# Accumulating SBUF-to-SBUF transfers described in pieces of 1024 bytes instead of 4096

## The chip, the cores and the metric

The kernel runs on one core of one Trainium2 chip. The metric is the device time of one execution in microseconds (us); the kernel before has a median of 198.1 us over 3 runs (198.0 to 198.31).

## What is computed

One transformer layer over 2048 positions of width 512, in bfloat16:

```
h  = x + A(layernorm(x))          # attention with 32 heads of 16
h2 = h + B(layernorm(h))          # gated MLP, 512 -> 1376 -> 512: (relu(gate) * up) @ W_down

A: q, k, v = x @ wqkv
   position s sees the 8 positions s, s-2, s-4, ..., s-14 (those below 0 are masked)
   logits[s, w] = q[s] . k[s - 2w] / 4 ;  attn = softmax over the 8 shifts w
   o[s] = sum over w of attn[s, w] * v[s - 2w] ;  A = o @ wo
```

The change touches the last sum, the one over the 8 shifts.

## The kernel before, in words

The positions are worked off in four chunks of 512 (tk = 0 to 3). For each chunk:

- Layer norm 1, transposes, and the projections to q, k and v (TensorE, L559), written transposed: partitions are features, so that k and v shifted by 2w positions are the same tile read from another column.
- Scores: VectorE multiplies q by four shifted k at a time (L608, a tile "big" of 128 x 8 x 512, 8 KB in a partition); TensorE adds over the features of a head (L614); ScalarE takes the exponent (L672).
- In chunks 1 to 3 the weights are divided by their sum (L716) and then spread to all features of a head by 8 transfers on SyncE's DMA queue, from tile ex to a big tile (L732). Chunk 0 spreads them with TensorE and ScalarE (L743, L749).
- The weighted values: for each of four feature groups t, VectorE multiplies the spread weights by the 8 shifted v into a big tile mt (L764; in two halves in chunk 0, L779).
- The sum over the 8 shifts, as a tree over mt: planes 4 to 7 are added to planes 0 to 3, then 2 and 3 to 0 and 1, then 1 to 0. In chunks 0, 1 and 2 (the set DACC, all four t) the first step isn't done by VectorE, but by a transfer that GpSimd issues and that adds while it moves (L807): 4 planes x 512 x 2 bytes, 4096 bytes in each of 128 partitions, 512 KB. There are 12 of them. The rest of the tree is on VectorE (L767), and its last step writes the attention output, tile quad (L801; in chunk 0 L767 and then L771, which multiplies by the reciprocal sum). In chunk 3 the whole tree is on VectorE.
- The output projection "wo" (TensorE, L833) needs all four groups t of the chunk. Then the residual (L844, or TensorE's L836 in chunk 0), layer norm 2, the MLP (L906 up and gate, L910 and L913 evictions, L934 the product, L952 down) and the stores.

The order of the work is fixed before it runs: a planner lists each step with its engine and an estimated cost, a table RANK gives each step its place, and every engine runs its list strictly in that order, waiting at each step for the semaphores of its inputs. MLP steps of one chunk fill TensorE's list between the attention steps of the next. For a step on a DMA queue the planner holds an estimate of its own; for the transfer of L807 it is 1.0 us of GpSimd and 2.74 us of the DMA engines. For a transfer twice as large in pieces of 4096 bytes, which the code has but doesn't use here, it is 1.3 us of GpSimd and 5.48 us of the DMA engines. These constants only set the order, and the change leaves them as they are.

There are 5 big tiles. A transfer reads and writes the same one.

Of the kernel before, what the change touches and what calls it, by code (L numbers as in the profile page):

```python
# [13 lines left out]
ALU = mybir.AluOpType  # L14
# [77 lines left out]
class Plan:  # L92
# [9 lines left out]
    def add(self, key, *a, **k):  # L102
        op = Op(*a, **k)
        op.key = key
        op.seq = len(self.ops)
        if RANK:
            op.prio = RANK[op.seq]
        self.ops.append(op)
        for b in set(op.take) | set(op.use):
            b.left += 1  # L110
        return op
# [97 lines left out]
def kernel(  # L209
# [11 lines left out]
    nc = tc.nc  # L221
# [320 lines left out]
    for tk in range(NCK):  # L542
# [213 lines left out]
        for t in range(NT):  # L756
            mt = Buf(big_s)
            tpr = apr + 3 + t

            def f_mu(t=t, ab=ab, mt=mt, s0=s0):  # L760
                vb = vT[:, t, PADL + s0: PADL + s0 + CS]
                v8 = bass.AP(tensor=vb.tensor, offset=vb.offset,
                             ap=[list(vb.ap[0]), [-DIL, W]] + [list(y) for y in vb.ap[1:]])
                V.tensor_tensor(out=mt.t[:], in0=ab.t[:], in1=v8, op=ALU.mult)  # L764

            def f_a(n, mt):
                V.tensor_tensor(out=mt.t[:, 0:n, :], in0=mt.t[:, 0:n, :], in1=mt.t[:, n:2 * n, :],  # L767
                                op=ALU.add)

            def f_om(t=t, mt=mt, rc=rc, OT=OT):  # L770
                V.tensor_tensor(out=OT.t[:, t, :], in0=mt.t[:, 0, :], in1=rc.t[:], op=ALU.mult)  # L771

            vds = [vd[t], kdone.get(("v", tk - 1, t))]
            if tk in MUH:
                def f_m1(hf, t=t, ab=ab, mt=mt, s0=s0):
                    vb = vT[:, t, PADL + s0 - 4 * hf * DIL: PADL + s0 - 4 * hf * DIL + CS]
                    v4 = bass.AP(tensor=vb.tensor, offset=vb.offset,
                                 ap=[list(vb.ap[0]), [-DIL, 4]] + [list(y) for y in vb.ap[1:]])
                    V.tensor_tensor(out=mt.t[:, 4 * hf:4 * hf + 4, :], in0=ab.t[:, 4 * hf:4 * hf + 4, :], in1=v4, op=ALU.mult)  # L779

                ms = [add(("mu%d%s" % (t, "ac"[hf]), tk), "DVE", D20, lambda hf=hf, f=f_m1: f(hf),
                          [x for x in abd if x.key[0][2] == str(hf)] + vds, tpr, take=[mt], use=[ab], lat=DL) for hf in range(2)]
            else:
                ms = [add(("mu%d" % t, tk), "DVE", D40, f_mu, abd + vds, tpr, take=[mt], use=[ab], lat=DL)]
            m = ms[-1]
            if (tk, t) in PESUM:
                u = Buf(od_s)

                def f_ac(mt=mt, u=u):
                    for w in range(W):  # L790
                        nc.tensor.matmul(u.t[:], lhsT=identity[:], rhs=mt.t[:, w, :],
                                         start=(w == 0), stop=(w == W - 1))

                def f_om(t=t, u=u, rc=rc, OT=OT):
                    V.tensor_tensor(out=OT.t[:, t, :], in0=u.t[:], in1=rc.t[:], op=ALU.mult)

                m = add(("ac%d" % t, tk), "PE", 8 * MM, f_ac, [m], tpr, take=[u], use=[mt], lat=PEL)
                oev[t] = add(("om%d" % t, tk), "DVE", D5, f_om, [m, rcd], tpr, take=[OT], use=[u, rc], lat=DL)
                continue
            def f_al(t=t, mt=mt, OT=OT):  # L800
                V.tensor_tensor(out=OT.t[:, t, :], in0=mt.t[:, 0, :], in1=mt.t[:, 1, :], op=ALU.add)  # L801

            for n, du in ((4, D20), (2, D10), (1, D2)):
                f = lambda n=n, mt=mt, f=f_a: f(n, mt)
                if n == 4 and (tk, t) in DACC:
                    def f_da(mt=mt):
                        nc.gpsimd.dma_start(mt.t[:, 0:4, :], mt.t[:, 4:8, :], accum_op=ALU.add)  # L807

                    ms = [m] = [add(("ta%d" % t, tk), "POOL", 1.0, f_da, ms, tpr, use=[mt], lat=1.1, dq=(0.75, 2.74))]
                    continue  # L810
                if n == 2 and (tk, t) in DAC2:
                    def f_db(mt=mt):
                        nc.gpsimd.dma_start(mt.t[:, 0:2, :], mt.t[:, 2:4, :], accum_op=ALU.add)

                    ms = [m] = [add(("tb%d" % t, tk), "POOL", 0.95, f_db, ms, tpr, use=[mt], lat=1.1, dq=(0.75, 1.37))]
                    continue
                if n == 1 and tk in EARLY:
                    oev[t] = add(("tree%d" % t, tk), "DVE", du, f_al, ms, tpr, take=[OT], use=[mt], lat=DL)
                else:
                    ms = [m] = [add(("tree%d" % t, tk), "DVE", du, f, ms, tpr, use=[mt], lat=0.11)]  # L820
            if tk not in EARLY:
                oev[t] = add(("om%d" % t, tk), "DVE", D2, f_om, [m, rcd], tpr, take=[OT], use=[mt, rc], lat=DL)
# [199 lines left out]
```

## Time and profile before

| | |
|---|---|
| median of 3 runs | 198.1 us |
| span of the profiled execution, first to last instruction | 196.6 us |
| what lies around the span, against the median | 1.5 us |
| TensorE (PE) matmul busy | 190.5 us (97%) |
| VectorE (DVE) busy | 154.0 us (78%) |
| ScalarE (ACT) busy | 111.7 us (57%) |
| GpSimd (POOL) busy | 12.7 us (6%), 10.5 of it the 12 instructions of L807 |

The profile holds no time of its own for the profiled execution beyond its span; the 1.5 us between the span and the median of the runs are start and end, outside of what it records.

How to read the lines of the profile: each names a line of the kernel (L807), the engine, the operation, and "tile written <- tile read" with the numbers of the buffers left out. PE is the matmul side of TensorE, PEld its weight loads. POOL's busy time for a transfer is only the time that GpSimd takes to write its list of pieces (its descriptors); the data moves afterwards on 16 DMA engines, which are shared by the queue of GpSimd (q0) and the queue of SyncE (q1). "Landing" is the moment when the last of the 16 engines has reported the end. A note in square brackets at the end of a line is the time for which the engine sat idle before it, and what it waited for.

### The profile page before, as it was taken

Reading aid. Unit: us, or ns where it says so; the run is one execution under the profiler, and the core shown is the slowest. Engines: PE = TensorE matmul, PEld = TensorE weight load, DVE = VectorE, ACT = ScalarE, POOL = GpSimd, SP = SyncE. Lnnn points to the kernel's source line nnn. Section 1 sums busy time; section 2 is a strip of 40 time slices with the busy share of each in tenths; the row PEclk is TensorE's granted clock in tenths of the full one; section 3 lists DMA queues with packets and bytes.
Section 4 is the critical chain, followed back from the end, with each engine's and each line's share of the span. In section 5 each row is a group of like instructions: output and inputs, shape, how many; then the busy total and the mean of one; then the engine's idle time right before and its main releaser. Section 6 shows DMA issues by size and latency. Waiting matters only on the chain.

```text
span 196.6 us, 3034 instructions
## 1 busy us (share of the span) xinstructions
PE 190.5 (97%) x1111; PEld 97.1 (49%) x1131; DVE 154.0 (78%) x251; ACT 111.7 (57%) x234; POOL 12.7 (6%) x28
## 2 busy tenths in 40 slices
PE   7899999999999999999999999999999999999994
PEld 7756445654445434464444435444444655444542
DVE  6779999999999999999999779999686331223233
ACT  3548699984598947694334658505674615235400
POOL 4000000330000013100033000000000000000000
PEclk9999999999999999999999999999999999999999
DMA  6969980695000809947369971411002220030114
GB/s 154 310 202 389 405 262 2 122 198 108 3 0 6 196 15 173 188 89 169 81 130 198 181 204 64 82 29 24 3 0 53 53 57 0 0 107 0 27 57 133
DMA packets 21134, 21.99 MB, mean 112 GB/s; under 512 B 8736, under 2 KB 17920, under 8 KB 21120
## 3 DMA queue, kind: packets, MB, share of 16 engines
q1 hardware_dynamic: 18672, 14.65, 25.9%
q0 software_dynamic: 1728, 6.29, 17.2%
q10 hardware_dynamic: 720, 0.85, 1.4%
q8 instruction: 9, 0.15, 0.3%
q14 instruction: 5, 0.04, 0.1%
HBM read 8.42 MB, written 2.10 MB: 53 GB/s over the span
## 4 chain that ended last, share of the span: by engine, by line
PE 66%; DMA 14%; issue 13%; DVE 4%; POOL 1%; SPq 1%; POOLq 0%; DVEq 0%
PE bank L906 20%; PE bank L559 19%; PE bank L952 14%; DMA big<-big 7%; PE bank L833 5%; DMA wv_sb<-in_A_wqkv_dram 4%; PE bank L614 2%; DVE big L764 2%; PE bank L873 2%; PE bank L518 2%; DMA x_sm<-in_A_x_dram 1%; POOL big L807 1%; DMA big<-ex 1%; DVE big L608 1%; PE bank L836 1%
## 5 line engine op out<-in xcount | busy, mean ns | idle before, releaser
L906 PE MATMUL bank<-quad,wgu_sb 128*128 128x512 bf16 x313 | 72.0, 379 | 0.4
L906 PEld LDWEIGHTS <-wgu_sb 128*128 128x128 bf16 x320 | 31.0, 98 | 37.3 <-issue 0.8
L952 PE MATMUL bank<-wd_sb,gT 128*128 128x512 bf16 (+2 forms) x182 | 40.1, 366 | 0.3
L913 ACT ACTIVATE gr<-bank 128x512 bf16<-128x512 f32 x40 | 23.2, 603 | 26.0 <-PE bank L906 24.5
L910 ACT CAST up_sb<-bank 128x512 bf16<-128x512 f32 x40 | 23.2, 594 | 16.5 <-PE bank L906 14.0
L934 DVE TENSOR_TENSOR gT<-gr,up_sb 128x1024 bf16<-128x1024 bf16 x20 | 13.7, 689 | 22.7 <-ACT up_sb L910 16.8
L559 PE MATMUL bank<-quad,wqk_sb 128*128 128x512 bf16 (+1 forms) x132 | 30.2, 367 | 0.2
L952 PEld LDWEIGHTS <-gT 128*128 128x128 bf16 (+1 forms) x187 | 18.1, 98 | 19.5 <-issue 0.4
L764 DVE TENSOR_TENSOR big<-big,vT 128x4096 bf16<-128x4096 bf16 x12 | 27.0, 2283 | 0.1
L608 DVE TENSOR_TENSOR big<-quad,kT 128x4096 bf16<-128x4096 bf16 x12 | 27.0, 2284 | 0.0
L559 PEld LDWEIGHTS <-wqk_sb 128*128 128x128 bf16 x136 | 14.7, 114 | 13.0 <-issue 2.1
L963 DVE TENSOR_TENSOR row<-x_sm,bank 128x512 bf16<-128x512 bf16 (+1 forms) x17 | 10.8, 651 | 9.2 <-PE bank L952 9.2
L767 DVE TENSOR_TENSOR big<-big 128x1024 bf16<-128x1024 bf16 (+2 forms) x24 | 16.8, 729 | 1.2 <-DMA big<-big 1.2
L559 PE MATMUL bank<-quad,wv_sb 128*128 128x512 bf16 x62 | 15.7, 380 | 0.4 <-DMA wv_sb<-in_A_wqkv_dram 0.3
L807 POOL DMA_DIRECT2D big<-big x12 | 10.5, 874 | 85.0 <-DVE big L764 55.0
L833 PE MATMUL bank<-wo_sb,quad 128*128 128x512 bf16 x62 | 14.7, 379 | 0.4 <-DVE quad L801 0.3
L489 DVE TENSOR_SCALAR row<-x_sm,mv,rs 128x512 bf16<-128x512 bf16 x32 | 11.4, 407 | 1.8 <-ACT rs L471 1.8
L534 ACT COPY quad<-bank 128x1024 bf16<-128x1024 bf16 (+1 forms) x11 | 10.0, 944 | 4.5 <-PE bank L518 4.4
L567 ACT CAST kT<-bank 128x512 bf16<-128x512 f32 x16 | 8.9, 598 | 5.7 <-PE bank L559 5.5
L454 DVE BATCH_NORM_STATS2 st<-x_sm 128x6 f32<-128x512 bf16 x16 | 10.3, 675 | 2.1 <-DMA x_sm<-in_A_x_dram 2.1
L567 ACT CAST quad<-bank 128x512 bf16<-128x512 f32 x16 | 9.5, 607 | 3.6 <-PE bank L559 3.6
L443 ACT ACTIVATE row<-x_sm,mv 128x512 bf16<-128x512 bf16 x12 | 8.6, 714 | 4.2 <-DVE mv L435 4.0
(72 smaller groups left out, 157.5 us busy)
## 6 DMA issues: line engine op xcount, KB each, us to landing
big<-big POOLq DMA_DIRECT2D x12, 512.0 KB, 5.4
big<-ex SPq DMA_DIRECT2D x24, 128.0 KB, 2.7
out_dram<-row SPq DMA_DIRECT2D x15, 128.0 KB, 1.8
x_sm<-in_A_x_dram SPq DMA_DIRECT2D x3, 512.0 KB, 4.9
wgu_sb<-in_B_W_up_dram SPq DMA_DIRECT2D x1, 1376.0 KB, 8.8
wgu_sb<-in_B_W_gate_dram SPq DMA_DIRECT2D x1, 1376.0 KB, 11.8
wd_sb<-in_B_W_down_dram SPq DMA_DIRECT2D x1, 1280.0 KB, 15.2
wqk_sb<-in_A_wqkv_dram SPq DMA_DIRECT2D x2, 256.0 KB, 6.9
```

The costliest lines, as they stand in the source:

```text
L559: nc.tensor.matmul(mm.t[:, lo:hi], lhsT=wv_sb[:, dt, t:D:NT] if c == 2 else wqk_sb[:, dt, c * D + t:(c + 1) * D:NT], rhs=xnT.t[:, dt, lo:h ...
L567: nc.scalar.copy(out=o, in_=mm.t[:])
L608: V.tensor_tensor(out=pb.t[:].rearrange("p (t w) s -> p t w s", t=2), in0=q4, in1=k4, op=ALU.mult)
L764: V.tensor_tensor(out=mt.t[:], in0=ab.t[:], in1=v8, op=ALU.mult)
L767: V.tensor_tensor(out=mt.t[:, 0:n, :], in0=mt.t[:, 0:n, :], in1=mt.t[:, n:2 * n, :], op=ALU.add)
L807: nc.gpsimd.dma_start(mt.t[:, 0:4, :], mt.t[:, 4:8, :], accum_op=ALU.add)
L833: nc.tensor.matmul(od.t[:], lhsT=OT.t[:, t, j * P:(j + 1) * P], rhs=wo_sb[:, t, :], start=(t == 0), stop=(t == NT - 1 and tk not in RPE))
L906: nc.tensor.matmul(mm.t[:fs, lo:hi], lhsT=wgu_sb[:, dt, g, ft * P: ft * P + fs], rhs=hnT.t[:, dt, lo:hi], start=(dt == 0), stop=(dt == NT ...
L910: nc.scalar.copy(out=ub.t[:fs, i, :], in_=um.t[:fs, :])
L913: nc.scalar.activation(out=gr.t[:fs, i, :], in_=gm.t[:fs, :], func=ACT.Relu)
L934: V.tensor_tensor(out=gt.t[:fs, 0:n, :], in0=gr.t[:fs, 0:n, :], in1=ub.t[:fs, 0:n, :], op=ALU.mult)
L952: nc.tensor.matmul(od.t[:, c0:c1], lhsT=gts[ft].t[:fs, ft % 2, j * P:(j + 1) * P], rhs=wd_sb[:fs, ft, c0:c1], start=(ft == 0), stop=(ft == ...
```

## The change

One argument is added to the transfer. Each partition's 4096 bytes are now described as four pieces of 1024 bytes, one plane each:

```
-                        nc.gpsimd.dma_start(mt.t[:, 0:4, :], mt.t[:, 4:8, :], accum_op=ALU.add)
+                        nc.gpsimd.dma_start(mt.t[:, 0:4, :], mt.t[:, 4:8, :], accum_op=ALU.add, max_dma_last_dim=1024)
```

The instructions of all engines and their order stay the same, except that each of the 12 transfers of GpSimd is written as 128 x 4 x 512 elements where it was 128 x 2048. So a transfer has 512 pieces instead of 128, 32 for each DMA engine instead of 8. The bytes, the sum and the buffers are the same. The other place in the code that passes max_dma_last_dim isn't used.

## The prediction

> **What bounds the kernel now.** I read the busy times first, then the chain that ended last, then the DMA queues, and then the timelines of POOL, DVE and PE around the 12 transfers. From the page:
>
> ```profile
> PE 190.5 (97%) x1111; PEld 97.1 (49%) x1131; DVE 154.0 (78%) x251; ACT 111.7 (57%) x234; POOL 12.7 (6%) x28
> ...
> DVE  6779999999999999999999779999686331223233
> ...
> q0 software_dynamic: 1728, 6.29, 17.2%
> ...
> PE 66%; DMA 14%; issue 13%; DVE 4%; POOL 1%; SPq 1%; POOLq 0%; DVEq 0%
> ...
> big<-big POOLq DMA_DIRECT2D x12, 512.0 KB, 5.4
> ```
>
> PE is the bound: it idles some 6 us of the span, so almost nothing can be won anywhere. But DVE is at nine tenths or more from about 15 to 105 us, so in that stretch it has no idle time in which to absorb a delay. All 12 transfers lie there: four each issued at 34.7 to 42.2, 73.0 to 80.2 and 99.1 to 105.7 us. From the chain in order of time, the last four:
>
> ```profile
> 105.74 8.28 DMA big<-big
> 114.02 0.02 issue
> 114.04 0.70 DVE big L767
> 114.75 0.02 issue
> 114.77 0.44 DVE quad L801
> 115.20 0.05 issue
> 115.25 2.55 PE bank L833 x11
> ```
>
> The reader sees the last transfer of chunk 2 issued at 105.74, landed 8.28 us later, the rest of its tree, and wo right behind. From the timelines of DVE and of PE:
>
> ```profile
> 114.04 0.69 DVE L767 TENSOR_TENSOR big<-big 128x1024 bf16<-128x1024 bf16 x1 [1.16 <-DMA big<-big]
> ...
> 115.25 3.63 PE L833 MATMUL bank<-wo_sb,quad 128*128 128x512 bf16 x15 [0.33 <-DVE quad L801]
> ```
>
> DVE waited 1.16 us for that landing and PE 0.33 us for DVE. So here a later landing is paid by PE one for one, and an earlier one wins at most 0.33 us.
>
> In the other two chunks nothing waits yet. The slack of each transfer is the start of the addition that reads it (DVE's single instructions) minus its landing:
>
> - chunk 0: landings 39.44, 42.23, 45.09, 47.90; additions 39.86, 44.47, 47.32, 48.26; slack 0.42, 2.24, 2.23, **0.36**
> - chunk 1: landings 77.53, 80.34, 83.17, 85.98; the last addition at 86.73, slack **0.75**; the others 2.3 or more
> - between DVE's last write of the attention output and wo on PE: chunk 0, 50.62 to 50.95; chunk 1, 88.08 to 88.61. PE adds 0.3 and 0.5 of slack.
>
> In these two chunks the landings are 2.8 to 2.9 us apart, while the issues are 2.0 to 2.9 apart: from the second on, each transfer starts as the one ahead ends (first packets at 36.29, 39.00, 41.64, 44.36 in chunk 0). So within a chunk the lateness of the transfers adds up, and the fourth has the least slack.
>
> **The change, part by part.** No instruction moves on any engine; no wait is added; POOL has nothing else to do in these stretches. Two costs change.
>
> *The data, d per transfer.* In the trace's packet records an accumulating 4096-byte piece took 327 ns at the least and 340 in the median; 8 per engine and one completion of 21 ns make 2.74 us, close to the spacing seen. Plain pieces on q1 took 159 ns for 4096 bytes, 84 for 2048, 46 for 1024: a straight line of 36.8 ns per 1024 bytes and 8 to 9 ns for each piece. The 327 ns are two such readings of 4096 bytes (2 x 151) plus 26 ns. That part is paid for each piece, so a 1024-byte piece should take 2 x 37.7 + 26 = 101 ns, and with the median's 4% on top 105; 32 of them make 3.24 to 3.36 us, against 2.74: d = 0.5 to 0.6. Bounds by the nearest rows: two plain pieces of 1024 bytes, 92 ns, 2.94 us, d = 0.2; and, as the far end, the mean instead of the median of the 1024-byte pieces that spread the weights (69 ns with nothing else moving from 62 to 70 us), 2 x 69 + 26 = 164 ns, d = 2.5. Those read the same source four times over, which the transfers here don't; I take d = 0.56. Below nothing: 4 pieces can't beat two plain readings of 4096 bytes, 318 ns, so d is not under -0.18.
>
> The Trainium skill, in "DMA: Bandwidth & Descriptors", section "Why small descriptors are slow (HBM only)", speaks against this term: "SBUF↔SBUF transfers don't suffer this penalty". By that d is 0; the 46 ns for 1024 bytes against 159 for 4096 say that a fixed part of 8 ns is there on SBUF-to-SBUF pieces too, but no accumulating piece of 1024 bytes is in the trace.
>
> *The list of pieces, G.* POOL was busy 0.862 us for each list, and the first data moved 1.43 us after the start of the first list of chunks 1 and 2, thus 0.57 after its end. How much of the 0.862 goes with the number of pieces no row shows, as all 12 lists have 128. Bounds: nothing, if all of it is fixed; 3 x 0.862 = 2.59 us, if all goes with the count. The planner's own costs in the code are 1.0 us for 128 pieces and 1.3 for 256, thus 0.3 for 128 more; for 384 more that is G = 0.9, which I take. A list of 1.76 us still fits into the 2.0 to 2.9 us between issues, so G is paid once for each chunk, by its first transfer, and the others queue behind it.
>
> *The sum.* The fourth transfer of a chunk lands later by L = G + 4d = 0.9 + 2.24 = 3.14 us.
>
> - Chunk 0: DVE pays L - 0.36, about 2.8 (some of it at the first addition, 1.46 - 0.42, which also delays the fourth product by as much; the fourth transfer is queued anyway, so the sum is the same).
> - Chunk 1: the whole stretch is later by then; L - 0.75, about 2.4.
> - Chunk 2: nothing to absorb it, L, about 3.1.
>
> What one chunk leaves unused at wo on PE (0.3, 0.5) is gone at chunk 2, since there PE already waits for DVE, which carries all of it. Together 3L - 1.1 = 8.3 us. Behind chunk 2 no time is given back: PE is at nine tenths to the end and in a fixed order. Span 196.6 + 8.3 = 204.9; with the 1.5 around it, **206.4 us** against the median of 198.1.
>
> *The cover of everything else.* The SyncE queue shares the DMA engines: from 107 on the weights of chunk 3 are spread beside the third and fourth transfer of chunk 2, whose 16 completions were strewn from 111.49 to 113.66. Shorter accumulating pieces let q1 in more often. If its 32 pieces per engine (1.5 us) all go ahead, the fourth transfer loses up to 0.7 more; most of that is in the 2.2 us already, so I cost it at nothing. The reader of those weights (L764 at 119.92) isn't near wo.
>
> **The rivals.**
>
> - *Lists in proportion, 212.6 us.* With G = 2.59 POOL needs 3.45 us for a list, more than a transfer moves in 3.3, so the fourth list sets the fourth landing: 99.13 + 4 x 3.45 + 0.57 + 3.3 = 116.8, against 111.5 for the same point now, L = 5.2, 3L - 1.1 = 14.5. For it: GpSimd writes the list by program. Against: the planner's 1.0 and 1.3.
> - *Cheap pieces, 199.4 us.* G = 0 and d = 0.2 make L = 0.8: 0.4 in chunk 0, nothing left in chunk 1, 0.8 in chunk 2, 1.3 in all. For it: two readings explain all but 26 of 327 ns. With G = 0 and d = 0.56 it would be 203.7, between this and the forecast.
> - *No change, 198.1 us.* If the four pieces are joined again when the list is written, as they are contiguous in memory, or if reading them runs on without a gap, the fixed part is paid once for 4096 bytes, d = 0, and if the longer list costs nothing, L = 0. Against: every 1024-byte row on q1 is a packet of its own. The rule of the Trainium skill above, with the sentence of the same page's section "Anatomy of one DMA — SWDGE (gpsimd) path" that many descriptors can be emitted before the cost shows, gives this.
> - *Faster, 197.8 us.* Shorter pieces overlap better, one being read while the other is added: under 85 ns a piece, with G = 0, the sign turns. At the floor of 318 ns for four, L = -0.7; but only PE's 0.33 us at 115 wait for a landing at all, so that is all it wins. Place and price are bounded by that line of PE.
>
> **How the numbers follow.** Forecast, near 206.4 (204 to 210): 0.46. Lists in proportion or dearer pieces, around 212.6: 0.18. Cheap pieces, 199 to 204: 0.20. No change: 0.10. Faster: 0.06. A measurement of this kernel tells about 0.2%, 0.4 us, from no change; the fastest case is at that edge. So faster 0.05, within 0.2% 0.11, slower 0.84. The range leaves out the two last cases and a little above the list rival: 199.4 to 213.0.
>
> **What would show it.** The page's q0 line should have 512 x 12 data packets and 192 completions, 6336, and a share of 16 engines above 17.2% (about 20% of the longer span, at 105 ns a piece). POOL's L807 should take 1.7 to 1.9 us instead of 0.86; the first packet of a chunk should come by as much later. DVE's L767 should wait for "DMA big<-big" at the fourth transfer of every chunk, some 2.5 to 3 us each, where one wait of 1.16 stands now, and PE at wo for DVE quad. It is wrong if L807 stays at 0.86 us (then G = 0), if a piece takes much more than 105 ns, or if the packets stay at 1728. It is also wrong if DVE waits but PE does not: then PE had more work ready than its fixed order shows.

## The result, and the profile after

The kernel with 1024-byte pieces takes 205.32 us (median of 5 runs, 203.76 to 208.71) against 198.1: a ratio of 1.034, with a 95% interval of 1.0306 to 1.0373. The run at 208.71 us, at a mean granted clock of 0.975, is left out of the ratio. The forecast was 206.4. The profiled execution is the run at 203.76 us; its span is 202.0 us, 5.4 more than before.

From the page of the kernel after, the lines that answer to those shown of before:

```profile
PE 192.1 (95%) x1131; PEld 97.2 (48%) x1131; DVE 153.8 (76%) x251; ACT 111.9 (55%) x234; POOL 17.7 (9%) x28
...
DVE  6789999997999999969998749999966341023234
...
q0 software_dynamic: 6336, 6.29, 22.0%
...
PE 45%; DMA 22%; DVE 17%; issue 11%; POOL 2%; SPq 0%; POOLq 0%; DVEq 0%
...
L767 DVE TENSOR_TENSOR big<-big 128x1024 bf16<-128x1024 bf16 (+2 forms) x24 | 17.0, 731 | 7.9 <-DMA big<-big 7.9
L807 POOL DMA_DIRECT2D big<-big x12 | 15.5, 1295 | 83.4 <-DVE big L764 54.5
...
big<-big POOLq DMA_DIRECT2D x12, 512.0 KB, 7.1
```

The same 6.29 MB are 6336 packets instead of 1728, and a transfer lands 7.1 us after its issue instead of 5.4. The busy times of DVE and ACT are as they were. What is new stands in the last column of L767: 7.9 us of idle time before it, all waiting for the transfers (1.2 before), while POOL's lists grew by 5.0 us in all and POOL, busy for 9%, is nowhere near full. In the chain that ended last PE gives up a third of its share, and by its lines these transfers go from 7% to 16%.

The fourth transfer of each chunk, in the timeline of DVE of the kernel after (the note at the end is the idle time before the addition):

```profile
50.14 1.36 DVE L767 TENSOR_TENSOR big<-big 128x1024 bf16<-128x1024 bf16 x3 [1.37 <-DMA big<-big]
...
90.19 0.69 DVE L767 TENSOR_TENSOR big<-big 128x1024 bf16<-128x1024 bf16 x1 [1.59 <-DMA big<-big]
...
119.40 0.69 DVE L767 TENSOR_TENSOR big<-big 128x1024 bf16<-128x1024 bf16 x1 [2.72 <-DMA big<-big]
```

and wo behind it, in the timeline of PE:

```profile
52.56 1.04 PE L833 MATMUL bank<-wo_sb,quad 128*128 128x512 bf16 x4 [1.58 <-DVE quad L771]
...
91.28 3.53 PE L833 MATMUL bank<-wo_sb,quad 128*128 128x512 bf16 x15 [0.58 <-DVE quad L801]
...
120.61 3.63 PE L833 MATMUL bank<-wo_sb,quad 128*128 128x512 bf16 x16 [3.10 <-DVE quad L801]
```

wo of chunk 2 starts at 120.61 where it started at 115.25, 5.36 later, and the span is 5.38 longer: behind chunk 2 nothing is lost and nothing won back.

The fourth landing, counted from the first issue of its chunk (chunk 1: 85.98 - 73.00 before, 90.17 - 74.83 after), is later by 2.3 us in chunk 0, 2.36 in chunk 1 and 2.49 in chunk 2. Forecast was L = 3.14. From the fourth landings, 3L - 1.1 gives 6.1 us for the span; it grew by 5.4.

### The profile page after: what moved, and what is told of

Same layout as the page of the kernel before. It is cut to its first block, busy times and chain, and to the rows that moved or that the text cites. A ratio compares the mean times of both kernels' runs of the same rounds, so it can differ in the third digit from the quotient of the medians.

```text
span 202.0 us, 3054 instructions
## 1 busy us (share of the span) xinstructions
PE 192.1 (95%) x1131; PEld 97.2 (48%) x1131; DVE 153.8 (76%) x251; ACT 111.9 (55%) x234; POOL 17.7 (9%) x28
## 3 DMA queue, kind: packets, MB, share of 16 engines
q0 software_dynamic: 6336, 6.29, 22.0%
## 4 chain that ended last, share of the span: by engine, by line
PE 45%; DMA 22%; DVE 17%; issue 11%; POOL 2%; SPq 0%; POOLq 0%; DVEq 0%
PE bank L906 19%; DMA big<-big 16%; PE bank L952 14%; PE bank L833 5%; DMA x_sm<-in_A_x_dram 5%; DVE big L623 4%; DVE st L454 4%; PE bank L559 3%; DVE big L764 2%; DVE big L779 2%; PE bank L873 2%; POOL big L807 2%; DVE big L767 2%; DVE row L489 1%; DMA big<-ex 1%
## 5 line engine op out<-in xcount | busy, mean ns | idle before, releaser
L952 PE MATMUL bank<-wd_sb,gT 128*128 128x512 bf16 (+3 forms) x187 | 40.5, 367 | 0.0
L767 DVE TENSOR_TENSOR big<-big 128x1024 bf16<-128x1024 bf16 (+2 forms) x24 | 17.0, 731 | 7.9 <-DMA big<-big 7.9
L807 POOL DMA_DIRECT2D big<-big x12 | 15.5, 1295 | 83.4 <-DVE big L764 54.5
L833 PE MATMUL bank<-wo_sb,quad 128*128 128x512 bf16 x64 | 15.3, 380 | 5.3 <-DVE quad L801 3.7
L559 PE MATMUL bank<-quad,wv_sb 128*128 128x512 bf16 x64 | 15.8, 380 | 0.1
L833 PEld LDWEIGHTS <-quad 128*128 128x128 bf16 x64 | 6.0, 98 | 13.7 <-DVE quad L801 4.9
```

The costliest lines, as they stand in the source:

```text
L559: nc.tensor.matmul(mm.t[:, lo:hi], lhsT=wv_sb[:, dt, t:D:NT] if c == 2 else wqk_sb[:, dt, c * D + t:(c + 1) * D:NT], rhs=xnT.t[:, dt, lo:h ...
L833: nc.tensor.matmul(od.t[:], lhsT=OT.t[:, t, j * P:(j + 1) * P], rhs=wo_sb[:, t, :], start=(t == 0), stop=(t == NT - 1 and tk not in RPE))
L952: nc.tensor.matmul(od.t[:, c0:c1], lhsT=gts[ft].t[:fs, ft % 2, j * P:(j + 1) * P], rhs=wd_sb[:fs, ft, c0:c1], start=(ft == 0), stop=(ft == ...
```

## The experiments

**Piece size.** If the fixed part of a piece and the list set the price, 2048 bytes must cost much less than 1024, and 512 much more.

```
- ... accum_op=ALU.add, max_dma_last_dim=1024)
+ ... accum_op=ALU.add, max_dma_last_dim=2048)     # and 512
```

> Pieces of 2048 bytes in all 12 transfers. Theory (a list that grows by 0.42 us for 384 more pieces, 16.6 ns for each piece on an engine, lateness added up over four transfers, and PE paying it after small slacks): L807 takes about 1.0 us, the fourth landing is 0.14 + 4 x 0.13 = 0.7 us later, chunks 0 and 1 absorb nearly all of theirs, chunk 2 pays: 198.7 to 199.2 us. Rival (any description in less than whole rows costs the same, whatever the size): as with 1024 bytes, 203.5 to 205.5 us.

> Pieces of 512 bytes. Theory: 1024 pieces in a list, so L807 takes 0.86 + 7/3 x 0.42 = 1.84 us; a piece takes 78.7/2 + 16.6 = 56 ns, 64 of them 3.58 us, so d = 0.93 and L = 0.98 + 3.7 = 4.7 us; 3L - 1.1 = 13 us, 211 us, and PE idles over 3.4 us at wo of chunk 2 at least, so the granted clock should fall there in the profile and add 1 to 4 us: 211 to 215 us. Rival (cost in the length of the list alone, the DMA engines as fast with small pieces): 3 x 0.98 - 1.1, 200 us.

Measured: 199.74 us with 2048 bytes (ratio 1.0076, 1.0052 to 1.0100) and 221.34 with 512 (1.1146, 1.1092 to 1.1199). The packet records of the four kernels:

| bytes in a piece | shortest, median (ns) | list on POOL (us) | first landing of chunk 1 after its issue (us) | time (us) |
|---|---|---|---|---|
| 4096 | 327, 340 | 0.86 | 4.53 | 198.1 |
| 2048 | 176, 189 | 1.20 | 5.02 | 199.7 |
| 1024 | 101, 113 | 1.28 | 5.48 | 205.3 |
| 512 | 64, 74 | 1.55 | 6.93 | 221.3 |

The shortest pieces lie on the line of the forecast: 26 ns and 75 for each 1024 bytes give 326, 176, 101 and 64. The list does not grow in proportion: the step from one piece in a partition to two is 0.34 us, the next 256 pieces cost 0.08, the next 512 0.27. Both numbers for 2048 bytes are above what I expected, 0.14 us for the list and 198.7 to 199.2 for the time. The 512-byte kernel is dearer than either theory had it. Its page and its PE waits:

```profile
PEclk9999999999699999996999997699999999999999
...
q0 software_dynamic: 12480, 6.29, 26.6%
```

```profile
55.78 1.89 PE L833 MATMUL bank<-wo_sb,quad 128*128 128x512 bf16 x4 [4.16 <-DVE quad L771]
...
99.34 5.22 PE L833 MATMUL bank<-wo_sb,quad 128*128 128x512 bf16 x15 [3.98 <-DVE quad L801]
...
135.65 6.17 PE L833 MATMUL bank<-wo_sb,quad 128*128 128x512 bf16 x16 [6.30 <-DVE quad L801]
```

PE waits 4.16, 3.98 and 6.30 us at the three wo, and another 1.94 in chunk 2. About the end of each wait at wo the granted clock falls to half. The busy times by stretch of the same execution, for the three stretches that its clock record names (columns: stretch, length, busy time and instructions of PE, PEld, DVE, ACT and POOL, granted clock, DMA share, GB/s):

```profile
55.51:58.92 3.41, 3.14 (x8) 1.19 (x9) 3.41 (x3) 0.79 (x3) 0.00 (x0) 0.50 0.00 0
99.88:103.29 3.41, 3.41 (x9) 1.18 (x8) 2.70 (x10) 0.20 (x1) 0.00 (x0) 0.50 0.46 105
134.01:140.84 6.83, 5.19 (x13) 1.84 (x14) 3.90 (x10) 2.33 (x6) 0.00 (x0) 0.50 0.27 84
```

PE was busy in 11.7 of these 13.65 us; the rest is the end of two of the waits. At half clock the 11.7 us are 5.9 lost, beside 16.4 us of waits; with the 0.33 us waited before taken off, that is 21.9, and the span is 23.0 longer: 1.1 us are not traced. The waits themselves are longer than pieces of 56 ns give, because the 16 engines drift apart: the first engine finishes each transfer 3.6 us after the one ahead, 56 ns a piece, as expected, but the last engine is up to 2.3 us behind it in chunk 1, and up to 4.1 in chunk 2.

**One chunk against the others.**

```
+ kw = dict(max_dma_last_dim=1024) if tk == 2 else {}     # chunk2; tk < 2 in chunk01
```

> 1024-byte pieces only in the four transfers of chunk 2. Theory: no slack there, PE pays all of the lateness of the fourth landing, 2.2 to 2.5 us: 200.3 to 200.7 us, PE's wait at wo of chunk 2 near 2.8 us (0.33 before), no wait at chunks 0 and 1. Rival (each chunk's transfers cost the same, a third of the whole): 199.9 to 200.5 with the waits of all three alike; if chunk 2's loss came only from work that was late out of chunks 0 and 1, under 199 us.

> 1024-byte pieces in chunks 0 and 1 only, the complement of chunk2. Theory (lateness is paid where it arises, each chunk by its own slack): the waits of the kernel after at chunks 0 and 1, 1.6 us and 0.6 to 0.9 us on PE, and 0.3 to 0.4 at chunk 2 as before; wo of chunk 1 ends 2.5 to 2.7 us later and nothing more is added: 200.5 to 200.9 us, with no half clock as no wait reaches 3 us; together with chunk2's 2.3 to 2.8 us it makes the 5.4 to 5.7 of the whole change at full clock. Rival (chunk 2's wait absorbs what chunks 0 and 1 leave, or the other way round): the two parts make clearly more than 6 us, or one of them alone almost the whole.

Measured: chunk2 201.64 us (1.0170, 1.0121 to 1.0219), chunk01 201.28 (1.0154, 1.0132 to 1.0175). PE's waits, of chunk2 and then of chunk01:

```profile
117.28 3.63 PE L834 MATMUL bank<-wo_sb,quad 128*128 128x512 bf16 x16 [3.02 <-DVE quad L801]
```

```profile
52.15 1.04 PE L834 MATMUL bank<-wo_sb,quad 128*128 128x512 bf16 x4 [1.43 <-DVE quad L771]
90.85 3.53 PE L834 MATMUL bank<-wo_sb,quad 128*128 128x512 bf16 x15 [0.58 <-DVE quad L801]
117.54 3.63 PE L834 MATMUL bank<-wo_sb,quad 128*128 128x512 bf16 x16 [0.46 <-DVE quad L801]
```

Each chunk pays its own lateness, where it arises: the waits of the whole change stand in the two halves, 1.43 and 0.58 against 1.58 and 0.58, 3.02 against 3.10. Both times are above what was expected, chunk01 a little (201.28 against 200.5 to 200.9), chunk2 by 1 us (201.64 against 200.3 to 200.7). Chunk 2 alone had runs at 200.42 and 201.08 us with a mean granted clock of 1.000 and runs at 202.19 and 202.96 with 0.991 and 0.990. The same split stands in the runs of the kernel after: 203.76 with 0.998, and 204.93, 205.32 and 205.49 with 0.991 or 0.992. One stretch of 3.41 us at half clock takes 1.7 us, which is about the distance between the groups (1.2 to 1.7 us in the kernel after, 1.1 to 2.5 in chunk2).

**Is it the clock?** PE's wait at wo of chunk 2 was filled with 12 matmuls whose result is overwritten.

```
+                if tk == 2 and j == 0:            # fill; fill2: in whichever of the four groups goes first
+                    for _ in range(12):
+                        nc.tensor.matmul(od.t[:], lhsT=warm[:], rhs=wo_sb[:, 0, :], start=True, stop=True)
```

> The kernel after, with 12 matmuls of 512 columns (0.216 us each, 2.6 us in all, their result is overwritten) ahead of wo of chunk 2, in the wait for the fourth transfer. Theory that the runs at 204.9 to 205.5 us with a mean granted clock of 0.991 to 0.992 are runs in which the clock fell after PE's long wait: all runs at a clock near 0.998 and 203.6 to 204.0 us. Rival (the clock falls for another reason, or the difference comes from the transfers): the median stays near 205.3 us with clocks of 0.991.

This one missed its aim: the planner runs the group j = 0 last, so the 12 matmuls came behind the wait, not into it. PE still waited (3.13 us), the 2.6 us were added, 207.86 us, and the runs still fell apart into 206.0 and 207.07 at a clock of 0.999, 207.69 to 208.25 at 0.991 or 0.992, and 209.67 at 0.984. Put into the first group:

> The kernel after, with 12 matmuls of 512 columns (2.6 us, result overwritten) now ahead of the first of the four wo groups of chunk 2, thus in PE's wait of 3.1 us for the last landing. Theory (some runs lose a stretch of 3.41 us at half clock, 1.7 us, because PE idles about 3 us there): the groups of runs at clock 0.998 and 0.991 become one, at a clock of 0.998 to 1.0, and the median falls from 205.3 to 203.5 to 204.2 us. Rival (the clock falls for another reason): two groups as before, median 205 us or above.

Measured: 203.62 us (1.0281, 1.0259 to 1.0302), all five runs between 203.50 and 204.25, all at a clock of 1.000. PE of fill2:

```profile
116.92 2.75 PE L836 MATMUL bank<-wo_sb,warm 128*128 128x512 bf16 x12
120.36 3.63 PE L838 MATMUL bank<-wo_sb,quad 128*128 128x512 bf16 x16 [0.69 <-DVE quad L801]
```

wo starts no sooner, but the split is gone, and 1.7 us with it. So of the 7.2 us, 5.5 are waits and 1.7 are half clock, in most of the runs though not in the profiled one. One rival is left untested: fill2, and with it chunk01 above and dve20_after below, which have no long wait, ran on another chip than fill and chunk2, which show the split, and no kernel with the wait of 3 us was run there. That the fill ended the split, and not the chip, is likely by the clock records below, but not shown.

The Trainium skill, "TensorE: Matmul & The Clock Gate", "Part 1: The HAM clock gate", has the clock drop to half after an idle window of about 3.4 us that runs free of the kernel, so that a wait near that length may or may not meet it. This agrees with the stretches of 3.41 us in the 512-byte kernel, and with waits of 3.0 to 3.1 us that cost the clock in some runs only. The clock records show more of it. In the 512-byte kernel every change of the clock lies a whole number of steps of 3.413 us behind the moment at which full clock was first granted (15, 16, 28, 29, 38 and 40 steps), and so it does in g_alone, a run described below (25, 26, 34 and 36). That first moment differs from run to run, from 3.95 to 6.65 us after the start. The clock fell at the end of a step in which PE had idled for all 3.41 us (four times) or for 2.88 (once, at 99.88 us), so less than a whole step is enough. In the profiled run of the kernel after, the border between two steps, at 119.13 us, cuts the wait of 3.10 us into 1.63 and 1.48, and the clock stayed; in those of chunk2 and fill at most 1.95 us lie in one step. By these figures a wait of 3 us can cost the clock or not, by where it falls on the steps. No trace was kept of a run with 1024 bytes in which the clock fell.

**The list or the data?** The first transfer of a chunk shows its list, the last one hides it behind the transfers ahead.

```
+ kw = dict(max_dma_last_dim=1024) if t == (3, 3, 2)[tk] else {}     # first; (0, 2, 0) in last
```

> 1024-byte pieces only in the first transfer of each chunk. Theory: this one pays the longer list too (0.42 us) and its own data (0.4 to 0.55): all four landings are 0.8 to 1.0 us later. The first addition of chunk 0 waits 0.4 to 0.5 us, chunk 1 absorbs nearly all, chunk 2 pays 0.8 to 1.0: 198.9 to 199.4 us. Rival (each transfer costs a twelfth of the whole wherever it stands): 198.1 + 3/12 x 5.7 = 199.5 us, the same as for the last ones alone.

> 1024-byte pieces only in the last transfer of each chunk. Theory: its list is written while the transfer ahead is still moving, so only its data counts: landings 0.4 to 0.6 us later, chunk 0 pays 0.1, chunk 1 nothing, chunk 2 0.4 to 0.6: 198.5 to 198.8 us, less than with the first ones alone. Rival (a twelfth each): 199.5 us.

Measured: first 198.56 us (1.0023, 1.0010 to 1.0036), last 198.83 (1.0035, 1.0023 to 1.0047). The intervals overlap, and the order I expected isn't there. Neither is a twelfth of the whole for each transfer, which would be 199.5. In the trace of last, the one transfer in small pieces lands 0.4, 0.5 and 0.6 us later after its issue than before, chunk by chunk: d is about 0.5. In the trace of first, the first landing is 0.95 us late (list and data). The fourth, counted from the first issue of its chunk, is late by 0.74, 0.59 and 0.18 us in chunks 0, 1 and 2: the three transfers behind, in large pieces, make up between a fifth and four fifths of it.

The list alone, first with a copy and a fill, then with a fill that writes into the product itself:

```
+ if t == (3, 3, 2)[tk]:
+     nc.gpsimd.tensor_copy(out=warm[0:1, 0:1], in_=mt.t[0:1, 0, 0:1])     # g_alone
+     nc.gpsimd.memset(warm[:, 1:P], 0.0)
...
+     nc.gpsimd.memset(mt.t[:, 0, :], 0.0)                                  # g_write
```

> Pieces of 4096 bytes as before; ahead of the first list of each chunk GpSimd has a small copy and a fill of 128 x 127 to do (0.3 to 0.4 us), behind the product that the transfer waits for. It is the longer list without the smaller pieces. Theory: every landing of a chunk is 0.3 to 0.4 us later; chunks 0 and 1 absorb it (slack 0.36 and 0.75), chunk 2 pays it: 198.3 to 198.5 us. Rival (the list is what costs, the data hardly): three times 0.4 and more, 199.3 us or above.

g_alone says nothing on the list: 215.57 us. Its POOL timeline:

```profile
33.59 0.23 POOL L809 COPY warm<-big 1x1 bf16<-1x1 bf16 x1 [23.89 <-DVE big L780]
...
72.28 9.99 POOL L809 COPY warm<-big 1x1 bf16<-1x1 bf16 x1 [29.85 <-DVE big L765]
...
106.64 6.58 POOL L809 COPY warm<-big 1x1 bf16<-1x1 bf16 x1 [20.56 <-DVE big L765]
```

The copy of one element took 0.23 us in chunk 0, but 9.99 and 6.58 in chunks 1 and 2, and all lists of the chunk stood behind it.

> Pieces of 4096 bytes; ahead of the first list of each chunk GpSimd fills the first plane of that product with zeros (128 x 512, 0.4 to 0.45 us, it only writes), so the first list is late by about what the longer list of the kernel after takes (0.42 us), and the pieces stay large. One plane of one group in chunks 0 to 2 is left out of the sum by this. Theory that the list is the smaller part: first landings 0.4 us later, last ones 0.2 to 0.4, chunk 2 pays it: 198.3 to 198.5 us. Rival (the list carries half of the loss or more): 199.5 us and above.

Measured: 198.71 us (1.0036, 1.0021 to 1.0052). In chunks 1 and 2 the first list was late by 0.59 us against the second (1.86 and 1.61 us apart, where it was 2.45 and 2.20), rather more than the 0.42 of the kernel after; in chunk 0 only by 0.22 (2.17 against 2.39). The fourth landing, from its own issue, is later by 0.22, 0.27 and 0.02 us in the three chunks: all of it is left in chunk 0, half in chunk 1 and next to nothing in chunk 2. PE's wait at chunk 2 is 0.35 us against 0.33. The time is 0.2 to 0.4 above the expectation, the span only some 0.2 us above that of before (196.4 to 196.6 in most runs, against 196.3 in the middle of the runs of before beside them); where the rest outside the span comes from no run tells. The rival, that the list carries half of the loss, falls: with its lists late by 0.22 to 0.59 us, g_write costs 0.6 us in all.

**The last landing of chunk 2.** Its transfer is taken out, and DVE does that addition.

```
- DACC = tuple((k, t) for k in range(3) for t in range(4))
+ DACC = tuple((k, t) for k in range(3) for t in range(4) if (k, t) != (2, 0))
```

> The kernel before (4096 bytes), with the first step of the sum of chunk 2's last group on VectorE (1.22 us) instead of the transfer that lands last. The reading that an earlier landing there wins at most PE's wait of 0.33 us: DVE trades 1.16 + 0.87 us of idle time for 1.22 us of work and writes the attention output some 0.5 to 1 us sooner; 197.6 to 198.0 us. Rival (DVE's later evictions in 105 to 110 us hold PE up): 198.1 or slower. A few matmuls of the MLP get other banks of PSUM by this.

> The kernel after (1024 bytes), with the first step of the last group of chunk 2 on VectorE (1.22 us) instead of the transfer that lands last. Theory (PE's loss at chunk 2 is the fourth landing alone): chunks 0 and 1 cost 2.5 to 2.7 us as before, at chunk 2 the third landing comes some 4.7 us ahead of the fourth and PE waits little or not at all: 200.3 to 201 us, no half clock. Rival (DVE's own lateness holds wo up as much): 203 us and above.

Measured: with 4096 bytes 197.64 us (0.9975, 0.9965 to 0.9985), a little faster than the kernel before; with 1024 bytes 200.93 (1.0150, 1.0121 to 1.0179), against 205.32. The page of the first, and wo of chunk 2 in it and in the second:

```profile
PE 191.3 (98%) x1131; PEld 97.3 (50%) x1131; DVE 154.9 (79%) x252; ACT 111.7 (57%) x234; POOL 11.8 (6%) x27
```

```profile
114.45 3.62 PE L833 MATMUL bank<-wo_sb,quad 128*128 128x512 bf16 x16
```

```profile
117.73 3.63 PE L833 MATMUL bank<-wo_sb,quad 128*128 128x512 bf16 x16 [0.33 <-DVE quad L801]
```

In the first, no wait is noted before wo. In the second, of PE's 3.10 us 0.33 are left, and what remains of the loss is that of chunks 0 and 1, as in chunk01.

## Why the forecast held, point by point

- *What bounds the kernel.* Right. DVE had next to no idle time in the stretch of the transfers (0.6 us of it are found below), and PE paid in each chunk what was above its slack. That an earlier landing could win at most PE's 0.33 us at wo of chunk 2 agrees with dve20: with that transfer gone, 0.44 us against the runs of before beside it, 0.3 to 0.7 by the interval.
- *d, the data.* Right in mechanism and near in size. A piece was to take 101 ns at the least; it took 101. The median was 113 against 105 forecast. One transfer in small pieces lands 0.4 to 0.6 us later (last); d was 0.56. But the times of the pieces don't simply add up, as the forecast had it: 32 x 113 ns are 3.6 us, but in chunk 1 the first of the DMA engines to finish ended its transfers 3.04 to 3.07 us apart (2.62 to 2.73 before), and the last one 3.3 in the mean. So the records of neighbouring pieces overlap. Two details of the working were wrong. The line through the plain pieces has 37.7 ns for each 1024 bytes, as the sum then uses, not 36.8. And its 2048- and 4096-byte pieces are the loads of the weights wqk_sb and wo_sb from DRAM (at 3.5 to 8.9 and 15.8 to 17.5 us); of the plain pieces only those of 1024 bytes move from SBUF to SBUF, so the fixed part of 8 ns was not shown for SBUF to SBUF.
- *G, the list.* Mis-sized. The step "thus 0.3 for 128 more; for 384 more that is G = 0.9" came from the planner's costs; the list took 1.28 us, 0.42 more. And "G is paid once for each chunk, by its first transfer, and the others queue behind it" holds only in part: in g_write the fourth landing kept all of the late list in chunk 0, half in chunk 1 and almost none in chunk 2. Where it was made up, the transfers behind the late one were packed closer (2.9, 2.6 and 2.6 us apart in chunk 1 of g_write, where it was 2.8 each), so what I took for a full queue had up to 0.2 us to spare in a transfer. L was 2.3 to 2.5 us, and not 3.14. With the list as measured and d as in last, 0.42 + 4 x 0.5, it would be 2.4, and with no list and d = 0.56 it would be 2.2; how much of the list is left in the kernel after, no run shows.
- *The sum.* 3L - 1.1 with the measured L is 6.1; the span grew by 5.4, and fill2, whose clock is 1.000 in all runs, by 5.5 in time. Forecast 8.3. So 2.2 us of the difference are L. The other 0.6 to 0.7 fail, for the most part, at the step "What one chunk leaves unused at wo on PE (0.3, 0.5) is gone at chunk 2, since there PE already waits for DVE, which carries all of it": DVE didn't carry all of it. Behind wo of chunk 1 DVE had to wait for PE before, at the residual (L844); in the kernel after it came late and didn't wait. Two lines of before, and one of after:

```profile
86.73 0.68 DVE L767 TENSOR_TENSOR big<-big 128x1024 bf16<-128x1024 bf16 x1
...
90.54 0.69 DVE L844 SCALAR_TENSOR_TENSOR x_sm<-x_sm,bank 128x512 bf16<-128x512 bf16 x1 [0.17 <-PE bank L833]
```

```profile
93.55 0.68 DVE L844 SCALAR_TENSOR_TENSOR x_sm<-x_sm,bank 128x512 bf16<-128x512 bf16 x1
```

DVE was 3.46 us late at the last addition of chunk 1 (90.19 against 86.73), 3.01 at this residual, and 2.87 at the first issue of chunk 2 (102.00 against 99.13). These 2.87 and the 2.49 of the fourth landing are the 5.36 us by which wo of chunk 2 is late. A small slip is in the 1.5 us around the span, which sets the profiled run of before against the median of all: within one run it is 1.7 to 1.8 us (203.76 - 202.0).
- *What I left out.* The clock. Nothing in the profile of before showed what a wait of 3 us on PE does, as its longest was 1.0 us. In most runs it costs 1.7 us more. The total came near the forecast because this missing term makes up for 1.7 of the 2.8 us by which the waits were forecast too long. That is luck: at full clock the kernel takes 203.6 to 203.8 us (fill2, the profiled run), below the 204 to 210 of the forecast, and where the prediction has "with G = 0 and d = 0.56 it would be 203.7".
- *The rivals.* Lists in proportion (212.6) fell with the 1.28 us on POOL. Cheap pieces (199.4) is about what 2048 bytes cost, not 1024, though without the clock its variant of 203.7 fits the size better than the forecast does. "No change" fell with 6336 packets and 101 ns each, and "faster" with 205.3 us. The rival of lists takes L = 5.2 where its own terms give 5.3.
- *The rule against the change.* The section "Why small descriptors are slow (HBM only)" of "DMA: Bandwidth & Descriptors" in the Trainium skill exempts SBUF-to-SBUF transfers. For accumulating ones the runs decide otherwise: 26 ns for each piece, 8% of a 4096-byte piece and 26% of a 1024-byte one.
- *The signs.* As named: 6336 packets, a share above 17.2% (22.0), the first packet of a chunk 0.42 us later, DVE's waits at the fourth transfers and PE's behind them. Not as named: L807 took 1.28 us and not 1.7 to 1.9, and DVE waited 1.37 and 1.59 us at the fourth transfers of chunks 0 and 1, not 2.5 to 3; only the 2.72 of chunk 2 is as said.
- *The SyncE queue.* I costed it at nothing, up to 0.7. The lateness at the fourth landing is 2.49 us in chunk 2 and 2.36 in chunk 1, where that queue moved nothing until 0.7 us before the landing: 0.1 us. "Shorter accumulating pieces let q1 in more often" did not show: in the kernel before, the first weights of chunk 3 were issued at 107.00 us and began to move 1.9 us later; in the kernel after they were issued at 109.86 and began to move 4.7 us later, at 114.59, as the third transfer of chunk 2 ended (114.69).

## What to carry to other kernels

A transfer that nothing waits for can still be short of slack: compare each landing with the start of its reader, and let the lateness of transfers that stand in one queue add up to the last of them. Take the fixed cost of a piece from the intercept of the sizes that the trace has; it predicted the shortest 1024-byte piece to the nanosecond, and the lateness of one transfer to about 0.1 us. And price a new wait of TensorE twice if it comes near 3 us, as these did: as the wait, and as half clock behind it, in part of the runs; with the wait filled by matmuls of no use the second part was gone.

## What the runs showed of the hardware that was not expected

- A GpSimd copy of a single element, 0.23 us in one place, took 9.99 and 6.58 us while DVE ran products without a pause, each with both inputs in SBUF. In chunk 1 the last of them ended at 82.22 and the copy at 82.27; in chunk 2 they ended at 113.18 and 113.22, and DVE went on with an addition that has one input in PSUM. In g_write a fill of 128 x 512, which only writes, took 0.52 us at the same places. The Trainium skill, "SBUF — State Buffer", "Who interferes with whom", says that a DVE instruction with two SBUF inputs contends with a GpSimd instruction that reads SBUF, and not with one that only writes it. That agrees; that it is the shared read port was not tried apart.
- The list on POOL grows by steps: 0.86, 1.20, 1.28 and 1.55 us for 128, 256, 512 and 1024 pieces.
- The 16 DMA engines drift apart within a chunk: at the fourth transfer of chunk 1 the last engine ended 0.5 us behind the first with 4096-byte pieces, 0.4 with 2048, 0.9 with 1024 and 1.9 with 512.
